# Loads of k, v and part of the weights moved from SyncE's DMA queue to GpSimd's own

## The chip, the cores and the metric

The kernel runs on one core of one Trainium2 chip. The metric is the device time of one execution in microseconds: 828.01 us is the median of three runs of the kernel before (825.59, 828.01 and 830.17 us). Engines are named as the profile names them: PE is TensorE's matmul, PEld its weight load, DVE is VectorE, ACT is ScalarE, POOL is GpSimd, SP is SyncE, which here does nothing but issue DMAs.

## The reference

Two stages follow each other. The first is attention with 4 batches, 12 heads, 448 positions and 64 elements for each head, with a mix over the heads ahead of the softmax and another behind it. The second is a feed-forward layer with a rational activation, on 1792 tokens (4 x 448), width 768 (12 x 64) and 2048 inner columns.

```
scores = einsum('bhij,hg->bgij', scale * (q @ k^T), w_pre)
attn   = softmax(scores)                      # over j
out    = einsum('bgij,..->', attn, w_post) @ v
h      = x @ w_in                             # x: out, heads side by side
g      = (a0 + a1 h + a2 h^2 + a3 h^3) / (1 + |b0||h| + |b1| h^2)
result = g @ w_out
```

The weights w_in and w_out are given as float64; the kernel turns each number into two float32 parts itself (high and low) with integer operations, in pieces of 128 x 384 numbers.

## The kernel before, in words

**Attention.** The 448 rows of a batch are cut into four tiles of 120 rows (one of them 88), 16 tiles in all. For a tile, six QK steps (line 498, one for each pair of heads) write the scores to PSUM, ACT and DVE copy them to SBUF buffers named st (line 238 on DVE and 236 on ACT; six buffers), and a DMA for each head, the shuffle d<-st (line 520, SP's queue), rewrites them so that a partition holds a row and a head. Every pair of ten-row blocks of a tile then makes a group, 92 groups in all, in this chain: the mix ahead of the softmax on PE (line 599, needs all shuffles of the tile); the row maximum nm on DVE (line 605); the exponentials e on ACT (line 614); a guard on POOL that adds 1e-9 to the sums sm (line 621); the reciprocal rr on DVE (line 625); the scaling of the second mixing matrix, krs, on POOL (line 634, two for each group); the mix behind the softmax on PE (line 674), two groups later; and transposes on DVE (line 690). Three times for each tile PE multiplies with v (line 739). The results go to xs and by DMA to x_scr (line 762).

**Weights during attention.** The feed-forward weights with f = 0, 1 and 3 (the list VIA) are prepared while attention runs, 12 pieces: a load cr<-in_w (line 406), steps on ACT, POOL and DVE that write cm, cg and co, and a store w_scr<-co (line 450). The other weights are prepared later, during the feed-forward stage, by the same function put_w.

**Feed-forward.** 64 units of 18 matmuls (line 918), the activation on ACT and DVE, and 18 matmuls (line 1008).

**What sets the order.** A planner (class Plan) places every operation on an engine by assumed durations, due times (at), earliest times (since) and dependencies; the instructions are then issued in that order on each engine, and each engine runs its own list in order. In this planner a DMA on SP has a short duration there and a transfer time (extra) on one queue that serves one transfer after another. All loads and stores but 24 joins of the feed-forward output (line 1059, POOL) and three shuffles (ACT) are issued by SP. SP runs its list in order as well: a load that stands ahead of a shuffle is issued ahead of it.

**Names and lines that the change touches.** The function bulk (line 357) adds a load to the plan; put_k (line 368) loads k of a batch in 6 pieces of 224 KB; put_w (line 401) loads and prepares weights; put_v (line 707) loads v of a batch in four pieces (384 KB, the last one 192 KB). k and v have two buffers each, cr three.

Of the kernel before, what the change touches and what calls it, by code (L numbers as in the profile page):

```python
# [11 lines left out]
I32 = mybir.dt.int32  # L12
# [6 lines left out]
B, H, S, D = 4, 12, 448, 64  # L19
# [18 lines left out]
CV = 384  # L38
# [16 lines left out]
class Plan:  # L55
# [163 lines left out]
def dma(nbytes):  # L219
    return nbytes / 300e3  # L220
# [21 lines left out]
def mixed_attention_then_rational_ffn(ctx: ExitStack, tc, q, k, v, w, wmix, mask, a, b2, out):  # L242
# [3 lines left out]
    nc = tc.nc  # L246
# [5 lines left out]
    add = plan.add  # L252
# [6 lines left out]
    base, after = ctx.enter_context(ExitStack()), ctx.enter_context(ExitStack())  # L259
# [9 lines left out]
    def open_pools(stack, side, sizes):  # L269
# [32 lines left out]
    tau = [T0]  # L302
# [3 lines left out]
    first = {}  # L306
# [61 lines left out]
    def put_k(b, parts, at, gap=0.8):  # L368
        free = R["k"].take()
        n = H // 2 // parts  # L370

        def load(i):
            def fn():
                if i == 0:
                    K[b] = sb["k"].tile([128, H // 2, S], F32, tag="k", name="kk")
                nc.sync.dma_start(out=K[b][:, i * n:(i + 1) * n], in_=k[b, :, i * n:(i + 1) * n])
            return fn

        k_ld[b] = []
# [8 lines left out]
    VIA = (0, 1, 3)  # L388
# [11 lines left out]
    def put_w(f, c, at, since=0.0, g=None):  # L400
# [2 lines left out]

        def load():
            t = sb["cr"].tile([128, CV, 2], I32, tag="cr", name="cr")
            nc.sync.dma_start(out=t.rearrange("p n t -> p (n t)"), in_=w[f, :, sl].bitcast(I32))
            box["hi"], box["lo"] = t[:, :, 1], t[:, :, 0]

        def mag():
# [39 lines left out]
        def store():  # L449
            nc.sync.dma_start(out=w_scr[f][:, :, sl], in_=box["o"].bitcast(F32))  # L450

        ld = add("sp", 0.45, load, [R["cr"].take()], at=at - 5.0, extra=dma(128 * CV * 8), since=max(since, at - 9.0))
        near = lambda i, k: [] if g is None else [posts[min(g + i, len(groups) - 1)][k]]
        o1 = add("act", act(CV), mag, [ld, R["cm"].take(), *near(0, 3)], at=at, late=4.0)
        o2 = add({"dve": 0.32} if g is None else {"pool": 1.54}, 0, clamp, [o1, *near(0, 1)], at=at)
# [251 lines left out]
    def put_v(b, at, gap=8.0):  # L707
        def load(j):
            def fn():
                if j == 0:  # L710
                    V[b] = sb["v"].tile([128, NB, G6, D], F32, tag="v", name="vv")
                sl = slice(j, min(j + 2, NB))
                nc.sync.dma_start(out=V[b][:, sl], in_=v[b, :, sl])
            return fn

        free = R["v"].take()
        v_ld[b] = []
        for i, j in enumerate(range(0, NB, 2)):
            v_ld[b].append(bulk(
                0.63, load(j), [free], after=v_ld[b][:1], at=at + gap * i, nbytes=128 * min(2, NB - j) * G6 * D * 4, since=at + gap * i))  # L720

    Xs, sums = {}, {}

# [76 lines left out]
    for T in range(3, NT):  # L800
        put_q(T, at=tau[first[T - 1]] - LEAD.get(T, 22.0), since=tau[first[T - 1]] - LEAD.get(T, 22.0))
    for b in range(1, B):
        put_k(b, 6, at=tau[first[4 * b - 4]] + 20.0 if b > 1 else tau[first[2]] - 10.0, gap=7.0 if b > 1 else 4.5)
    for b in range(B):
        put_v(b, at=tau[first[4 * b - 4]] + 58.0 if b else 23.0, gap=7.0 if b else 0.7)
    for pr in range(H // 2):
# [353 lines left out]
```

## Time and profile before

| what | value |
|---|---|
| median of 3 runs | 828.01 us (825.59 to 830.17) |
| the profiled execution | 822.94 us, of which the span (first to last instruction) is 821.2 us |
| granted TensorE clock, mean | 0.998 of full speed |
| busy in the span | PE 97%, PEld 73%, DVE 84%, ACT 61%, POOL 27% |
| attention (20 to 340 us) and feed-forward (340 us to the end) | 320 us and 481.2 us |

PE's busy time includes matmuls that run into one another, so a busy PE is not PE at its best rate. A row of the timeline stands for several like instructions in a row: its start and length in us, then in brackets the idle time ahead of it and what ended that.

### The profile page before, as it was taken

What the parts mean: (1) busy time and instruction counts of PE and PEld (TensorE: products, weight loads), DVE (VectorE), ACT (ScalarE), POOL (GpSimd) and SP (SyncE); (2) the same over time, 40 slices, a digit from 0 to 9 for tenths busy, and PEclk for the clock granted to TensorE, in tenths of its full rate; (3) what the DMA queues carried; (4) which work ended last, traced back from release to release, by engine and by line L of the source; (5) the groups of instructions that cost most, each with busy time, mean ns of one, the idle gap of its engine ahead of it and who ended that gap; (6) DMA issues with size and microseconds to landing.
All of it is one profiled execution on the core that took longest, in us unless ns stands there. A gap on an engine that the chain in (4) does not pass through costs nothing.

```text
span 821.2 us, 23269 instructions
## 1 busy us (share of the span) xinstructions
PE 799.4 (97%) x9368; PEld 598.1 (73%) x9368; DVE 692.3 (84%) x1252; ACT 502.0 (61%) x1099; POOL 223.7 (27%) x394
## 2 busy tenths in 40 slices
PE   7899999999999999999999999999999999999998
PEld 2245555554454454689999999999999999999997
DVE  6777788888887888788999998999989998777775
ACT  2557666656665666666777776677657676545632
POOL 2334444434343445611211212222212222100000
PEclk9999999999999999999999999999999999999999
DMA  6777887668877865974733275656467534466314
GB/s 219 254 215 235 259 280 236 209 199 281 266 212 210 269 192 189 352 243 192 257 126 100 75 255 126 188 124 125 84 215 212 152 81 67 94 221 224 128 52 157
DMA packets 72332, 155.46 MB, mean 189 GB/s; under 512 B 12608, under 2 KB 53152, under 8 KB 71072
## 3 DMA queue, kind: packets, MB, share of 16 engines
q1 hardware_dynamic: 68468, 142.47, 52.6%
q0 software_dynamic: 3456, 11.01, 8.2%
q8 instruction: 74, 1.21, 0.6%
q10 hardware_dynamic: 300, 0.48, 0.2%
q14 instruction: 34, 0.28, 0.1%
HBM read 77.49 MB, written 37.75 MB: 140 GB/s over the span
## 4 chain that ended last, share of the span: by engine, by line
PE 87%; DVE 5%; DMA 3%; ACT 2%; issue 1%; POOL 1%; SPq 0%; ACTq 0%; POOLq 0%; DVEq 0%
PE ps_s L918 29%; PE ps_u L1008 10%; PE ps_t L1008 9%; PE ps_a L1008 9%; PE ps_s L498 8%; PE ps_a L674 8%; PE ps_u L599 4%; PE ps_t L599 4%; PE ps_u L739 3%; PE ps_t L739 2%; ACT e L614 2%; DVE nm L605 2%; DMA d<-st 1%; DVE aa L690 1%; DMA kk<-in_k 1%
## 5 line engine op out<-in xcount | busy, mean ns | idle before, releaser
L690 DVE STREAM_TRANSPOSE aa<-ps_a 128x448 f32<-128x448 f32 (+1 forms) x184 | 107.7, 618 | 11.7 <-PE ps_a L674 11.2
L918 PE MATMUL ps_s<-d,w 128*128 128x448 f32 x504 | 107.3, 366 | 0.0
L918 PE MATMUL ps_s<-xs,w 128*128 128x448 f32 x504 | 107.1, 366 | 0.0
L447 POOL TENSOR_TENSOR w<-cm,w 128x384 fp32r<-128x384 f32 x48 | 56.0, 1167 | 171.9 <-ACT w L236 165.0
L918 PEld LDWEIGHTS ps_s<-d,w 128*128 128x128 f32 x504 | 94.3, 188 | 8.8 <-issue 0.7
L918 PEld LDWEIGHTS ps_s<-xs,w 128*128 128x128 f32 x504 | 94.6, 188 | 7.9
L634 POOL TENSOR_SCALAR krs<-kpost,rr 128x64 f32<-128x64 f32 x180 | 80.8, 462 | 69.2 <-DVE rr L625 48.0
L674 PEld LDWEIGHTS ps_a<-e,krs 64*32 64x32 f32 x2880 | 44.9, 106 | 74.7 <-issue 26.6
L674 PE MATMUL ps_a<-e,krs 64*32 64x224 f32 x2880 | 93.2, 355 | 1.5 <-DVE aa L690 0.8
L236 ACT COPY st<-ps_s 120x448 f32<-120x448 f32 (+1 forms) x115 | 57.6, 533 | 57.8 <-PE ps_s L498 30.5
L931 ACT ACTIVATE m<-ps_s,a_sb 128x448 f32<-128x448 f32 x64 | 46.3, 723 | 76.1 <-PE ps_s L918 72.7
L498 PE MATMUL ps_s<-kk,q 64*64 64x448 f32 x696 | 90.2, 548 | 0.3 <-DVE st L238 0.3
L1008 PE MATMUL ps_u<-g,w 128*128 128x448 f32 x336 | 84.1, 366 | 0.0
L1008 PE MATMUL ps_a<-g,w 128*128 128x448 f32 x336 | 84.1, 366 | 0.0
L1008 PE MATMUL ps_t<-g,w 128*128 128x448 f32 x336 | 83.9, 366 | 0.0
L614 ACT ACTIVATE e<-ps_t,nm 128x448 f32<-128x448 f32 x92 | 57.7, 634 | 31.1 <-DVE nm L605 28.0
L614 ACT ACTIVATE e<-ps_u,nm 128x448 f32<-128x448 f32 x88 | 55.2, 633 | 28.9 <-DVE nm L605 24.6
L1008 PEld LDWEIGHTS ps_t<-g,w 128*128 128x128 f32 x336 | 63.1, 188 | 5.3
L1008 PEld LDWEIGHTS ps_a<-g,w 128*128 128x128 f32 x336 | 63.1, 188 | 5.2
L1008 PEld LDWEIGHTS ps_u<-g,w 128*128 128x128 f32 x336 | 63.1, 188 | 5.2
L961 DVE TENSOR_TENSOR sq<-sq,ua 128x448 f32<-128x448 f32 x64 | 41.4, 648 | 19.4 <-ACT ua L958 19.1
L954 ACT ACTIVATE ua<-sq 128x448 f32<-128x448 f32 x64 | 37.1, 580 | 33.9 <-DVE sq L951 33.6
(94 smaller groups left out, 1445.1 us busy)
## 6 DMA issues: line engine op xcount, KB each, us to landing
d<-st SPq DMA_DIRECT2D x144, 210.0 KB
cr<-in_w SPq DMA_DIRECT2D x64, 384.0 KB
d<-x_scr SPq DMA_DIRECT2D x5, 2688.0 KB
xs<-x_scr SPq DMA_DIRECT2D x4, 2688.0 KB
o_scr<-o POOLq DMA_DIRECT2D x24, 448.0 KB, 5.5
d<-st SPq DMA_DIRECT2D x45, 157.5 KB
x_scr<-xs SPq DMA_DIRECT2D x12, 540.0 KB
q<-in_q SPq DMA_DIRECT2D x16, 384.0 KB
```

Of the source, the lines that this page charges most:

```text
L236: eng.copy(o, i)
L447: eng.tensor_sub(t[:, 1, :], box["m"].bitcast(F32), t[:, 0, :].bitcast(F32))
L498: nc.tensor.matmul(box["s"][hh][i0:i1, 0:S], lhsT=Q[T][d, pr, i0:i1], rhs=K[b][d, pr, :], start=True, stop=True)
L599: nc.tensor.matmul(box[r if nt == 2 else 0]["t"][64 * c:64 * c + 64, 0:S], lhsT=kpre[p], rhs=Dt[T][p, kb + c if nt == 2 else kb, :], start ...
L614: nc.scalar.activation(e, box[r]["t"][:, 0:S], AF.Exp, bias=box[0]["nm"][:, r:r + 1], accum_out=box[0]["sm"][:, r:r + 1])
L634: eng.tensor_scalar_mul(box[r]["kr"], kpost, rr)
L674: nc.tensor.matmul(banks[c]["p"][q_:q_ + BT, JH * r:JH * (r + 1)], lhsT=box[r]["kr"][p, m_, :], rhs=box[r]["e"][p, JH * jh:JH * (jh + 1)], ...
L690: nc.vector.transpose(o, src)
L918: nc.tensor.matmul(h[:, 0:S], lhsT=W[fi][:, wi, kk * 128:(kk + 1) * 128], rhs=x[:, kk // 3, xj, kk % 3, :], start=(n == 0), stop=(n == 3 * ...
L931: nc.scalar.activation(new("m"), box["h"], AF.Identity, scale=a_sb[:, 3:4], bias=a_sb[:, 2:3])
L961: nc.vector.tensor_mul(box["vv"], box["vv"], box["rc"])
L1008: nc.tensor.matmul(O[key][:, 0:S], lhsT=W[fi][:, wi, DM + m * 128:DM + (m + 1) * 128], rhs=box["g"][:, gi, :], start=(f == 0 and n == 0), ...
```

## The change

The pieces of k of batches 1 to 3, those of v of batches 1 to 3, and the loads of the 12 weight pieces that are prepared during attention are issued by GpSimd (nc.gpsimd.dma_start) and no longer by SyncE. k of these batches comes in 3 pieces of 448 KB in place of 6 of 224 KB. The planner is told 1.0 us on POOL and 4 us more until the data is there. 33 DMAs are added to POOL's list (9 of k, 12 of v, 12 of weights), and 42 leave SP's list (18, 12 and 12). Batch 0's k and v, and all weights loaded in the feed-forward stage, stay on SP.

```
--- before.py
+++ after.py
@@ -356,6 +356,8 @@
 
     def bulk(dur, fn, deps, at, nbytes, **more):
 
+        if more.pop("by", "sp") == "pool":
+            return add("pool", 1.0, fn, deps, at=at, extra=4.0 + dma(nbytes), **more)
         return add("sp", dur, fn, deps, at=at, extra=dma(nbytes), **more)
 
     def put_q(T, at, since=0.0):
@@ -373,12 +375,12 @@
             def fn():
                 if i == 0:
                     K[b] = sb["k"].tile([128, H // 2, S], F32, tag="k", name="kk")
-                nc.sync.dma_start(out=K[b][:, i * n:(i + 1) * n], in_=k[b, :, i * n:(i + 1) * n])
+                (nc.gpsimd if b else nc.sync).dma_start(out=K[b][:, i * n:(i + 1) * n], in_=k[b, :, i * n:(i + 1) * n])
             return fn
 
         k_ld[b] = []
         for i in range(parts):
-            k_ld[b].append(bulk(0.45, load(i), [free], at=at + gap * i, nbytes=128 * n * S * 4, since=at + gap * i - 4.0, after=k_ld[b][:1]))
+            k_ld[b].append(bulk(0.45, load(i), [free], at=at + gap * i, nbytes=128 * n * S * 4, since=at + gap * i - 4.0, after=k_ld[b][:1], by="pool" if b else "sp"))
 
 
     w_done = {f: [] for f in range(NF)}
@@ -403,7 +405,7 @@
 
         def load():
             t = sb["cr"].tile([128, CV, 2], I32, tag="cr", name="cr")
-            nc.sync.dma_start(out=t.rearrange("p n t -> p (n t)"), in_=w[f, :, sl].bitcast(I32))
+            (nc.gpsimd if f in VIA else nc.sync).dma_start(out=t.rearrange("p n t -> p (n t)"), in_=w[f, :, sl].bitcast(I32))
             box["hi"], box["lo"] = t[:, :, 1], t[:, :, 0]
 
         def mag():
@@ -449,7 +451,7 @@
         def store():
             nc.sync.dma_start(out=w_scr[f][:, :, sl], in_=box["o"].bitcast(F32))
 
-        ld = add("sp", 0.45, load, [R["cr"].take()], at=at - 5.0, extra=dma(128 * CV * 8), since=max(since, at - 9.0))
+        ld = add("pool" if f in VIA else "sp", 1.0 if f in VIA else 0.45, load, [R["cr"].take()], at=at - 5.0, extra=(4.0 if f in VIA else 0.0) + dma(128 * CV * 8), since=max(since, at - 9.0))
         near = lambda i, k: [] if g is None else [posts[min(g + i, len(groups) - 1)][k]]
         o1 = add("act", act(CV), mag, [ld, R["cm"].take(), *near(0, 3)], at=at, late=4.0)
         o2 = add({"dve": 0.32} if g is None else {"pool": 1.54}, 0, clamp, [o1, *near(0, 1)], at=at)
@@ -710,14 +712,14 @@
                 if j == 0:
                     V[b] = sb["v"].tile([128, NB, G6, D], F32, tag="v", name="vv")
                 sl = slice(j, min(j + 2, NB))
-                nc.sync.dma_start(out=V[b][:, sl], in_=v[b, :, sl])
+                (nc.gpsimd if b else nc.sync).dma_start(out=V[b][:, sl], in_=v[b, :, sl])
             return fn
 
         free = R["v"].take()
         v_ld[b] = []
         for i, j in enumerate(range(0, NB, 2)):
             v_ld[b].append(bulk(
-                0.63, load(j), [free], after=v_ld[b][:1], at=at + gap * i, nbytes=128 * min(2, NB - j) * G6 * D * 4, since=at + gap * i))
+                0.63, load(j), [free], after=v_ld[b][:1], at=at + gap * i, nbytes=128 * min(2, NB - j) * G6 * D * 4, since=at + gap * i, by="pool" if b else "sp"))
 
     Xs, sums = {}, {}
 
@@ -800,7 +802,7 @@
     for T in range(3, NT):
         put_q(T, at=tau[first[T - 1]] - LEAD.get(T, 22.0), since=tau[first[T - 1]] - LEAD.get(T, 22.0))
     for b in range(1, B):
-        put_k(b, 6, at=tau[first[4 * b - 4]] + 20.0 if b > 1 else tau[first[2]] - 10.0, gap=7.0 if b > 1 else 4.5)
+        put_k(b, 3, at=tau[first[4 * b - 4]] + 20.0 if b > 1 else tau[first[2]] - 10.0, gap=14.0 if b > 1 else 9.0)
     for b in range(B):
         put_v(b, at=tau[first[4 * b - 4]] + 58.0 if b else 23.0, gap=7.0 if b else 0.7)
     for pr in range(H // 2):
```

The planner orders all engines anew. The order of PE's matmuls is the same before and after.

POOL's list at the groups 8 to 12 (kk and in_k are k, cr and in_w the weights, sm the guard, krs the scaling); before:

```order
L621 TENSOR_SCALAR sm<-sm 128x2
L634 TENSOR_SCALAR krs<-kpost,rr 128x64 x2
L621 TENSOR_SCALAR sm<-sm 128x2
L634 TENSOR_SCALAR krs<-kpost,rr 128x64 x2
L621 TENSOR_SCALAR sm<-sm 128x2
L634 TENSOR_SCALAR krs<-kpost,rr 128x64 x2
L621 TENSOR_SCALAR sm<-sm 128x2
L634 TENSOR_SCALAR krs<-kpost,rr 128x64 x2
L337 MEMSET c_sb 128x1
```

The same groups on POOL in the changed kernel:

```order
L378 DMA kk<-in_k 128x896
L623 TENSOR_SCALAR sm<-sm 128x2
L636 TENSOR_SCALAR krs<-kpost,rr 128x64 x2
L623 TENSOR_SCALAR sm<-sm 128x2
L636 TENSOR_SCALAR krs<-kpost,rr 128x64 x2
L378 DMA kk<-in_k 128x896
L623 TENSOR_SCALAR sm<-sm 128x2
L636 TENSOR_SCALAR krs<-kpost,rr 128x64 x2
L337 MEMSET c_sb 128x1
```

Two DMAs of k stand between the scaling of a group and the guard of the next: the first ahead of the guard of group 9, the second ahead of that of group 11, the first of tile 2.

POOL's list at the groups 51 to 53 (tiles 8 and 9; cm is a step of the weights), before:

```order
L621 TENSOR_SCALAR sm<-sm 128x2
L416 TENSOR_SCALAR cm<-cm 128x384
L634 TENSOR_SCALAR krs<-kpost,rr 128x64
L621 TENSOR_SCALAR sm<-sm 128x2
L634 TENSOR_SCALAR krs<-kpost,rr 128x64 x3
L447 TENSOR_TENSOR co<-cm,co 128x384
L621 TENSOR_SCALAR sm<-sm 128x2
L634 TENSOR_SCALAR krs<-kpost,rr 128x64 x2
```

The same place on POOL in the changed kernel:

```order
L623 TENSOR_SCALAR sm<-sm 128x2
L378 DMA kk<-in_k 128x896
L418 TENSOR_SCALAR cm<-cm 128x384
L623 TENSOR_SCALAR sm<-sm 128x2
L636 TENSOR_SCALAR krs<-kpost,rr 128x64 x2
L408 DMA cr<-in_w 128x768
L636 TENSOR_SCALAR krs<-kpost,rr 128x64 x2
L623 TENSOR_SCALAR sm<-sm 128x2
```

A DMA of k now stands behind the guard of group 51, ahead of the step cm, and a load of weights between the scalings of the groups 51 and 52.

SP's list around the first loads of k of batch 1, before:

```order
L520 DMA d<-st 10x12x448 x3
L376 DMA kk<-in_k 128x448
L520 DMA d<-st 10x12x448 x2
L376 DMA kk<-in_k 128x448
L406 DMA cr<-in_w 128x768
L376 DMA kk<-in_k 128x448 x2
L520 DMA d<-st 10x12x448 x2
L364 DMA q<-in_q 128x768
```

The same place on SP in the changed kernel:

```order
L522 DMA d<-st 10x12x448 x5
L366 DMA q<-in_q 128x768
L522 DMA d<-st 10x12x448 x6
```

The shuffles of a tile now follow one another with nothing between them but a load of q.

## Rows read from the trace of the kernel before

**Rows 1.** The page's chain that ended last, by engine

```profile
PE 87%; DVE 5%; DMA 3%; ACT 2%; issue 1%; POOL 1%; SPq 0%; ACTq 0%; POOLq 0%; DVEq 0%
```

**Rows 2.** Busy time by stretch: length, each engine (instructions), clock, DMA share, GB/s

```profile
20.00:340.00 320.00, 308.14 (x6653) 154.98 (x6646) 262.64 (x484) 196.39 (x530) 134.98 (x303) 0.99 0.76 238
340.00:821.20 481.20, 477.36 (x2612) 438.09 (x2610) 416.70 (x750) 299.62 (x560) 83.16 (x82) 1.00 0.52 156
```

**Rows 3.** Timeline of PE, the mix ahead of the softmax: start, length, idle before

```profile
34.70 0.98 PE L599 MATMUL ps_t<-d,kpre 64*64 64x448 f32 x8 [2.49 <-DMA d<-st]
54.70 0.98 PE L599 MATMUL ps_u<-d,kpre 64*64 64x448 f32 x8 [0.30 <-DMA kk<-in_k]
138.29 0.98 PE L599 MATMUL ps_u<-d,kpre 64*64 64x448 f32 x8 [0.28 <-DMA cr<-in_w]
```

**Rows 4.** The chain of waits at 47 us: start, length, what

```profile
47.26 7.46 DMA kk<-in_k
```

**Rows 5.** Timeline of PE, QK steps of tiles 8 and 12

```profile
160.74 1.21 PE L498 MATMUL ps_s<-kk,q 64*64 64x448 f32 x8
167.34 1.85 PE L498 MATMUL ps_s<-kk,q 64*64 64x448 f32 x8
251.38 1.91 PE L498 MATMUL ps_s<-kk,q 64*64 64x448 f32 x8 [0.33 <-DVE st L238]
```

**Rows 6.** Timeline of ACT, a copy of scores

```profile
251.72 0.53 ACT L236 COPY st<-ps_s 120x448 f32<-120x448 f32 x1 [1.21 <-DMA d<-st]
```

**Rows 7.** Timeline of SP's queue

```profile
162.69 0.50 SPq L713 DMA_DIRECT2D vv<-in_v  x1
163.29 6.19 SPq L520 DMA_DIRECT2D d<-st  x6
```

**Rows 8.** Line 1059, DMAs issued by POOL: ns min/median/max; us to landing

```profile
L1059 POOL DMA_DIRECT2D o_scr<-o x24: 858/872/1063, 500.3 to 716.1; - x24
DMA to landing us min/median/max: 5.0/5.5/11.2
```

**Rows 9.** By line, 20 to 340 us: count | busy, mean ns | idle

```profile
L634 POOL TENSOR_SCALAR krs<-kpost,rr 128x64 f32<-128x64 f32 x177 | 79.0, 460 | 69.2 <-DVE rr L625 48.0 <-PE ps_a L674 9.1 <-PE ps_s L498 4.8
L621 POOL TENSOR_SCALAR sm<-sm 128x2 f32<-128x2 f32 (+1 forms) x90 | 20.9, 232 | 115.0 <-ACT e L614 113.0 <-PE ps_t L599 0.2
L238 DVE COPY st<-ps_s 120x448 f32<-120x448 f32 (+1 forms) x55 | 33.5, 617 | 12.7 <-PE ps_s L498 9.0 <-PE ps_a L674 3.2 <-DMA d<-st 0.2
```

**Rows 10.** Timeline of POOL: groups 10 and 11, group 24, group 51

```profile
57.60 0.86 POOL L634 TENSOR_SCALAR krs<-kpost,rr 128x64 f32<-128x64 f32 x2 [1.56 <-PE ps_a L674]
58.55 0.22 POOL L621 TENSOR_SCALAR sm<-sm 128x2 f32<-128x2 f32 x1
59.84 0.86 POOL L634 TENSOR_SCALAR krs<-kpost,rr 128x64 f32<-128x64 f32 x2 [1.07 <-DVE rr L625]
...
104.44 0.86 POOL L634 TENSOR_SCALAR krs<-kpost,rr 128x64 f32<-128x64 f32 x2 [0.83 <-DVE rr L625]
...
201.72 1.50 POOL L416 TENSOR_SCALAR cm<-cm 128x384 f32<-128x384 f32 x1 [0.22 <-ACT cm L411]
203.20 0.45 POOL L634 TENSOR_SCALAR krs<-kpost,rr 128x64 f32<-128x64 f32 x1
```

**Rows 11.** Timeline of DVE, reciprocal of group 11

```profile
59.53 0.14 DVE L625 RECIPROCAL rr<-sm 128x2 f32<-128x2 f32 x1
```

**Rows 12.** Timeline of PE, the mix behind the softmax of groups 11, 24, 51

```profile
61.53 0.99 PE L674 MATMUL ps_a<-e,krs 64*32 64x224 f32 x32
...
108.62 0.99 PE L674 MATMUL ps_a<-e,krs 64*32 64x224 f32 x32
...
204.48 1.42 PE L674 MATMUL ps_a<-e,krs 64*32 64x224 f32 x32
```

**Rows 13.** The page's DMA queues: packets, MB, share of 16 engines

```profile
q1 hardware_dynamic: 68468, 142.47, 52.6%
q0 software_dynamic: 3456, 11.01, 8.2%
```

More of the change, by code (lines that the diff above doesn't have):

```diff
@@ L357, in bulk @@
     def bulk(dur, fn, deps, at, nbytes, **more):
+        if more.pop("by", "sp") == "pool":
+            return add("pool", 1.0, fn, deps, at=at, extra=4.0 + dma(nbytes), **more)
         return add("sp", dur, fn, deps, at=at, extra=dma(nbytes), **more)
@@ L375, in fn @@
                     K[b] = sb["k"].tile([128, H // 2, S], F32, tag="k", name="kk")
-                nc.sync.dma_start(out=K[b][:, i * n:(i + 1) * n], in_=k[b, :, i * n:(i + 1) * n])
+                (nc.gpsimd if b else nc.sync).dma_start(out=K[b][:, i * n:(i + 1) * n], in_=k[b, :, i * n:(i + 1) * n])
             return fn
@@ L380, in put_k @@
         for i in range(parts):
-            k_ld[b].append(bulk(0.45, load(i), [free], at=at + gap * i, nbytes=128 * n * S * 4, since=at + gap * i - 4.0, after=k_ld[b][:1]))
+            k_ld[b].append(bulk(0.45, load(i), [free], at=at + gap * i, nbytes=128 * n * S * 4, since=at + gap * i - 4.0, after=k_ld[b][:1], by="pool" if b else "sp"))
     w_done = {f: [] for f in range(NF)}
@@ L405, in load @@
             t = sb["cr"].tile([128, CV, 2], I32, tag="cr", name="cr")
-            nc.sync.dma_start(out=t.rearrange("p n t -> p (n t)"), in_=w[f, :, sl].bitcast(I32))
+            (nc.gpsimd if f in VIA else nc.sync).dma_start(out=t.rearrange("p n t -> p (n t)"), in_=w[f, :, sl].bitcast(I32))
             box["hi"], box["lo"] = t[:, :, 1], t[:, :, 0]
@@ L450, in store @@
             nc.sync.dma_start(out=w_scr[f][:, :, sl], in_=box["o"].bitcast(F32))
-        ld = add("sp", 0.45, load, [R["cr"].take()], at=at - 5.0, extra=dma(128 * CV * 8), since=max(since, at - 9.0))
+        ld = add("pool" if f in VIA else "sp", 1.0 if f in VIA else 0.45, load, [R["cr"].take()], at=at - 5.0, extra=(4.0 if f in VIA else 0.0) + dma(128 * CV * 8), since=max(since, at - 9.0))
         near = lambda i, k: [] if g is None else [posts[min(g + i, len(groups) - 1)][k]]
@@ L712, in fn @@
                 sl = slice(j, min(j + 2, NB))
-                nc.sync.dma_start(out=V[b][:, sl], in_=v[b, :, sl])
+                (nc.gpsimd if b else nc.sync).dma_start(out=V[b][:, sl], in_=v[b, :, sl])
             return fn
@@ L719, in put_v @@
             v_ld[b].append(bulk(
-                0.63, load(j), [free], after=v_ld[b][:1], at=at + gap * i, nbytes=128 * min(2, NB - j) * G6 * D * 4, since=at + gap * i))
+                0.63, load(j), [free], after=v_ld[b][:1], at=at + gap * i, nbytes=128 * min(2, NB - j) * G6 * D * 4, since=at + gap * i, by="pool" if b else "sp"))
     Xs, sums = {}, {}
@@ L802, in mixed_attention_then_rational_ffn @@
     for b in range(1, B):
-        put_k(b, 6, at=tau[first[4 * b - 4]] + 20.0 if b > 1 else tau[first[2]] - 10.0, gap=7.0 if b > 1 else 4.5)
+        put_k(b, 3, at=tau[first[4 * b - 4]] + 20.0 if b > 1 else tau[first[2]] - 10.0, gap=14.0 if b > 1 else 9.0)
     for b in range(B):
```

## The prediction

> **What bounds the kernel now.** I read the chain that ended last first: PE holds 87% of the span, all DMAs together 3%, POOL 1% [rows 1]. Then the busy time by stretch [rows 2]: in the feed-forward stage PE is busy for 477 of 481 us, so what attention gains or loses arrives at the end unchanged. In attention, 20 to 340 us, PE is busy for 308.14 of 320 us: 11.9 us of pauses, and that is the room for any gain there, beside matmuls that are stretched without a pause in the profile. Then the timeline of PE, for which of these pauses have SP's queue behind them. The longest is 2.49 us, ahead of the mix of group 5, the first of tile 1, at 34.70 us, and it waits for a shuffle [rows 3]. It stands among batch 0's loads, where the order on SP is the same before and after, so it stays. Two more start a tile's mix late by 0.30 and 0.28 us and are put down to a load of k and one of the weights; what the mix needs is the tile's last shuffle, which landed with them on the same queue [rows 3]. The chain shows how long that queue is: a piece of k issued at 47.26 us landed 7.46 us later [rows 4]. Third, two QK steps late in a tile last 1.85 and 1.91 us where the one before lasts 1.21 [rows 5]; the ACT copy beside the second waits 1.21 us for a shuffle to release an st buffer [rows 6]. On SP one sees why: a load of v, then six shuffles that take 6.19 us to issue [rows 7].
>
> **The change part by part.**
>
> *Loads off SP.* 42 DMAs leave SP's list (18 of k, 12 of v, 12 of weights). With about 0.5 us for each [rows 7] SP has 21 us less to issue. SP's time is not on the chain (0%) [rows 1], so it counts only where a shuffle is late. Those places are: 0.30 at 54.70 us, 0.28 at 138.29 us, 1.85 - 1.21 = 0.64 at 167.34 us, and 1.91 - 1.21 + 0.33 = 1.03 at 251.38 us [rows 3, 5]. Sum 2.25 us. From above the gain is bounded by all pauses in attention without the one that stays, 11.9 - 2.5 = 9.4, and the two stretches, 0.64 + 0.70: 10.7 us. From below by nothing: the transfers still run on the DMA engines that the shuffles use, busy 76% in this stretch [rows 2], and a load that is served beside the shuffles may hold them up as much as one ahead of them. I take 2.25, since those rows name a DMA or the shuffle's buffer and the other pauses name ACT or DVE.
>
> The Trainium skill, "DMA: Bandwidth & Descriptors" (section "Issuing engines are not separate DMA queues"), says that DMAs from any engine run on the same 16 DMA engines and interleave, so that issuing from several engines saves only the issue time. By that rule the sum loses its 2.25 us and would be a loss of 1.3 us. The trace before cannot decide, since it has no stretch of attention with two queues at work.
>
> *Issues on POOL.* 33 DMAs are added. POOL's only DMAs in the trace, 24 joins of 448 KB, take 858 to 1063 ns of POOL each, median 872 [rows 8]; I take that for each of the 33, which makes 28.8 us. POOL idles for 320 - 135 = 185 us of attention [rows 2], mostly in front of the guard (115 us) and of the scaling (69 us) [rows 9]. So the question is only where an issue stands. A group's scaling has to be done before PE's mix behind the softmax. In wide groups there is room: group 24's scaling ends at 104.44 + 0.86 = 105.30 and PE comes at 108.62, 3.3 us later; in tight ones there is little: group 11's ends at 60.70, PE comes at 61.53, 0.8 us [rows 10, 12]. I went through POOL's new list group by group against the timeline of before: 28 of the 33 issues stand in wide groups, with 1.4 us or more to spare, and cost nothing. Five stand at tight ones.
>
> Group 11 is the pattern of four of them. The k load follows group 10's scaling (57.60 + 0.86 = 58.46) and ends at 59.33; the guard (0.22) then runs to 59.55 in place of 58.77. The reciprocal starts at 59.53 in any case [rows 11], since DVE had other work, so it moves by some 0.1 us, which the 0.8 us take up. I put 0.1 us on each, 0.4 in all. The fifth is group 51: the k load stands between its guard and the step cm, which runs from 201.72 to 203.22, with the scaling right behind it at 203.20 and PE at 204.48 already waiting (1.42 us in place of 0.99) [rows 10, 12]. There the whole 0.87 us goes on the path. Cost 1.3 us. The bounds: nothing, if every issue is hidden, and 5 x 1.06 = 5.3 us, if none of the five is.
>
> *Landing of the moved loads.* POOL's DMAs land 5.0 to 11.2 us after issue [rows 8]. The last piece of k of batch 1 is issued behind group 10 and first read at about group 16, six groups of 320 / 90 = 3.6 us later (90 guards in the stretch [rows 9]): 21 us, so it costs nothing; with that cover gone, PE would wait for all of it. The other k, v and weight loads have as many groups or more, and the buffers into which they go are free groups earlier, so that no issue waits on POOL.
>
> *The rest of the plan.* Larger pieces of k carry the same bytes. DVE takes 72 score copies in place of 70 and ACT two fewer; at 617 ns [rows 9] that is 1.2 us of DVE, which idles for 57 us of the stretch [rows 2]: taken at nothing, 1.2 us as its bound. In the feed-forward stage DVE and ACT get another order, behind a PE that never pauses there: nothing.
>
> *Sum.* -2.25 + 1.3 = -0.95 us. The profiled execution took 822.94 us, 821.2 of it span, and would take 822.0. It lies 5.1 us under the median of the runs, 828.01, so for the median I take 828.01 - 0.95 = 827.1 us. A difference under 0.5% (4.1 us) is about what a measurement of this kernel can't tell from none.
>
> **The rivals.**
>
> *Faster: the queue was behind more than the rows name.* Shuffles on time keep the st buffers free, and then ACT and DVE, which run their lists in order, are early as well. At most all 10.7 us go; with the 1.3 us on POOL that is 9.4 us, 818.6 us. For it: the 7.46 us from issue to landing [rows 4], and st buffers that are full in one place at least [rows 6]. Against it: most pauses in the timeline are put down to ACT or DVE and not to a DMA.
>
> *Slower: POOL in the chain.* The guard and the scaling of every group run on POOL; if an issue holds POOL longer than 0.87 us, the tight groups pay. Group 11 has 0.76 us up to its reciprocal and 0.8 us behind it, so an issue of up to 1.5 us is hidden there; group 51 pays at once. With no gain from SP and none of the five hidden it is 5.3 us, 833.3 us. For it: a POOL that lies between ACT's sums and DVE's reciprocal in every group, with DVE waiting in order behind it. Against it: 185 us idle, and 28 of 33 issues in wide groups. It decides from about 1.5 us for one issue.
>
> The Trainium skill, "SBUF — State Buffer" (sections "SBUF: two separate sides" and "A bandwidth-pool intuition that's wrong (but worth ruling out)"), warns that descriptors of DMAs from GpSimd are written by GpSimd itself, which VectorE's two-port operations lock out of the shared port: about 620 ns alone, 3100 ns beside such an operation. The rows agree only in part: beside a busy DVE the 24 joins spread by 0.2 us and not by 2.5 [rows 8]. Had each issue taken the page's 3.1 us, five tight places would pay some 5 x (3.1 - 1.5) = 8 us, an estimate.
>
> *Slower: busier DMA engines.* For each MB, POOL's queue took 8.2 / 11.01 = 0.74% of the engines' time and SP's 52.6 / 142.47 = 0.37% [rows 13]. The moved 13 MB at the first price add 4.9% of 821 us, 40 us, to a stretch of 320 us that stands at 76%: 88%. The shuffles then land later; if each of the 13 tile starts from tile 3 on waits as at 54.70 us, that is 13 x 0.30 = 3.9 us, and with 1.3 on POOL and no gain 833.2 us. Against it: the joins add in memory, which plain loads don't.
>
> *Nothing but a swap.* The engines serve the same bytes, and a shuffle waits beside a load in place of behind it: no gain, 1.3 us of cost, 829.3 us. This is within the same bound as the forecast.
>
> **How the numbers follow.** Forecast and swap together, from 823.9 to 832.1 us: 0.46. The faster rival, all beyond 4.1 us: 0.30, as the pauses leave room but name other engines. POOL in the chain 0.15, busier DMA engines 0.09, both slower by more than 0.5%. Range for 8 in 10: down to 819.0, near the end of the faster rival, and up to 833.5, just over the ends of the slower ones. Faster 0.30, same 0.46, slower 0.24; the likeliest case's own range is 823.9 to 832.1 us.
>
> **What would show it.** Right: the mixes at 54.70 and 138.29 us start without a pause that names a DMA, no QK step takes 1.8 us, DMA issues on POOL take about 0.87 us each, 33 of them, and PE's pauses from 20 to 340 us fall by about a microsecond. Wrong: POOL's issues at 1.5 us or more, PE waiting behind scalings at tight groups, shuffles landing later than before, or pauses that vanish where no DMA was named.

## The result and the profile after

The changed kernel is slower: 838.22 us against 828.46 us (medians of 16 runs each), ratio 1.0106, interval 1.008 to 1.0131. Ratios here are taken over undisturbed runs, so one can differ a little from the ratio of the two medians. The profiled execution has a span of 836.8 us, 15.6 us over the one before. Only part of that is the change: the execution before that was profiled took 822.94 us, 5.5 us less than its median. So where a term is read from these two traces it can be too large by half, and the runs below decide.

By stretch (length; busy us and instructions of PE, PEld, DVE, ACT, POOL; clock; DMA share; GB/s), the changed kernel, cut where the feed-forward stage starts in it:

```profile
20.00:355.60 335.60, 314.18 (x6654) 155.97 (x6655) 263.76 (x486) 195.94 (x528) 153.76 (x337) 0.98 0.73 227
355.60:836.80 481.20, 477.24 (x2612) 437.95 (x2610) 421.06 (x754) 297.73 (x556) 80.77 (x81) 1.00 0.52 155
```

Beside [rows 2], the feed-forward stage takes 481.2 us in both, so all 15.6 us are lost in attention. PE's pauses there are 335.60 - 314.18 = 21.4 us, in place of 11.9; the other 6.0 us are matmuls that last longer. The DMA engines are no busier: 0.73 of a longer stretch, in place of 0.76.

The longer matmuls go with TensorE's granted clock (the third number from the end of a row). It was below full speed in three stretches of 20 us of the changed kernel:

```profile
20.00:40.00 20.00, 17.83 (x224) 6.11 (x228) 13.28 (x24) 9.13 (x26) 5.24 (x15) 0.77 0.80 235
60.00:80.00 20.00, 19.95 (x416) 9.79 (x408) 14.87 (x28) 11.72 (x33) 9.89 (x21) 0.92 0.64 183
280.00:300.00 20.00, 17.85 (x396) 8.85 (x392) 14.67 (x29) 10.97 (x30) 8.15 (x17) 0.91 0.80 261
```

The kernel before had 0.91 in the first of these stretches and 1.00 in the other two:

```profile
20.00:40.00 20.00, 16.33 (x236) 5.64 (x228) 14.25 (x26) 10.13 (x29) 6.11 (x17) 0.91 0.77 253
```

A mean below 1.00 says that a part of the stretch ran at the lower of the clock's two levels, 1.2 GHz in place of 2.4. The differences make 20 x (0.14 + 0.08 + 0.09) = 6.2 us, an estimate, which is about the 6.0. The first 2.8 us of it are not the loads' doing: they stand ahead of the first moved load (42.93 us, shown below), and the kernel with v alone on GpSimd, which loses nothing, has 0.78 in that stretch. The other 3.4 us come after pauses of PE that the kernel before did not have, or had shorter (shown next).

The page's chain that ended last, by engine and by line:

```profile
PE 71%; DMA 5%; DVE 4%; issue 1%; ACT 1%; POOL 0%; SPq 0%; ACTq 0%; DVEq 0%; POOLq 0%
PE ps_s L920 28%; PE ps_u L1010 9%; PE ps_t L1010 9%; PE ps_a L1010 9%; DMA d<-st 5%; PE ps_a L676 4%; PE ps_s L500 3%; PE ps_u L741 2%; PE ps_u L601 2%; PE ps_t L601 2%; PE ps_t L741 2%; DVE nm L607 1%; ACT e L616 1%; DVE aa L692 1%; DVE xs L759 1%
```

Beside [rows 1] the DMAs' share went from 3% to 5% of a longer span, the whole 5% being shuffles, and POOL is at 0%. The chain's pieces (start, length) show single shuffles from issue to landing:

```profile
191.46 7.64 DMA d<-st
203.35 6.44 DMA d<-st
305.23 6.97 DMA d<-st
```

PE's timeline, pauses in attention, the changed kernel:

```profile
53.14 1.04 PE L741 MATMUL ps_u<-aa,vv 64*64 64x90 f32 x40 [1.56 <-issue]
...
58.86 0.98 PE L601 MATMUL ps_u<-d,kpre 64*64 64x448 f32 x8 [2.27 <-DMA d<-st]
...
201.03 0.98 PE L601 MATMUL ps_t<-d,kpre 64*64 64x448 f32 x8 [1.10 <-ACT e L616]
205.30 0.56 PE L741 MATMUL ps_u<-aa,vv 64*64 64x90 f32 x17 [0.95 <-issue]
209.98 0.98 PE L601 MATMUL ps_u<-d,kpre 64*64 64x448 f32 x8 [1.64 <-DMA d<-st]
214.47 1.03 PE L676 MATMUL ps_a<-e,krs 64*32 64x224 f32 x32 [0.17 <-POOL krs L636]
...
263.66 2.02 PE L500 MATMUL ps_s<-kk,q 64*64 64x448 f32 x8 [0.54 <-DVE st L238]
...
294.64 0.47 PE L741 MATMUL ps_t<-aa,vv 64*64 64x90 f32 x12 [2.15 <-issue]
...
351.47 0.47 PE L741 MATMUL ps_u<-aa,vv 64*64 64x120 f32 x9 [1.47 <-issue]
```

Three rows of the kernel before to set beside them:

```profile
196.61 0.54 PE L739 MATMUL ps_u<-aa,vv 64*64 64x90 f32 x16 [0.35 <-issue]
200.23 0.98 PE L599 MATMUL ps_u<-d,kpre 64*64 64x448 f32 x8 [0.57 <-DMA x_scr<-xs]
...
281.81 0.45 PE L739 MATMUL ps_t<-aa,vv 64*64 64x90 f32 x9 [1.59 <-issue]
```

The row at 58.86 us answers to the mix at 54.70 us in [rows 3]: it waited 0.30 us and now waits 2.27. At 209.98 us the first mix of tile 9 waits 1.64 us for a shuffle; before, at 200.23 us, it waited 0.57. These two are 3.0 us of the 9.5 us by which PE's pauses grew. A larger part, 4.2 us, stands in the middle of the v matmuls and waits for nothing that the profile shows ("issue"): 6.1 us in four pauses, in place of 1.9 in two. The DMA records of the two traces say more: each of these six pauses ends 1.3 to 1.7 us after the end of a transfer of 16 KB on q8, the queue that the page calls "instruction", so PE seems to have waited for its own instructions. Whether the moved loads delayed these transfers was not tested. The step of 1.91 us in [rows 5] is still there, at 2.02. Around the mix at 58.86 us, SP's queue and POOL:

```profile
42.72 5.64 SPq L522 DMA_DIRECT2D d<-st  x5
48.41 0.50 SPq L366 DMA_DIRECT2D q<-in_q  x1
56.30 1.66 SPq L522 DMA_DIRECT2D d<-st  x2
```

```profile
42.93 0.78 POOL L378 DMA_DIRECT2D kk<-in_k  x1
...
46.16 0.61 POOL L408 DMA_DIRECT2D cr<-in_w  x1
...
50.65 0.59 POOL L378 DMA_DIRECT2D kk<-in_k  x1
```

Five shuffles of tile 2 are issued from 42.72 to 48.36 us. Beside them POOL issues 448 KB of k and 384 KB of weights, and the mix that needs the last of these shuffles starts at 58.86 us, 10.5 us after its issue. In the kernel before, the last two shuffles of tile 2 were issued by 47.21 us, and the mix, which waited there too, came 7.5 us later, at 54.70:

```profile
45.54 1.67 SPq L520 DMA_DIRECT2D d<-st  x2
```

At tile 9, POOL issues a piece of k ahead of the tile's last six shuffles (POOL, then SP's queue):

```profile
194.51 0.61 POOL L378 DMA_DIRECT2D kk<-in_k  x1
```

```profile
196.83 7.53 SPq L522 DMA_DIRECT2D d<-st  x6
```

What the moved loads cost the two queues (packets, MB, share of 16 engines):

```profile
q1 hardware_dynamic: 62420, 129.49, 46.1%
q0 software_dynamic: 6048, 23.99, 13.8%
```

With [rows 13]: POOL's queue took 13.8% of 836.8 less 8.2% of 821.2 = 48.1 us more of the engines for 12.98 MB, SP's 52.6% of 821.2 less 46.1% of 836.8 = 46.2 us less for the same 12.98 MB. A byte costs the engines almost the same on both, so the loss is not in their load. Last, the landing of the nine loads of k, and all issues on POOL, 20 to 355.6 us (count, busy us, mean ns, idle before):

```profile
DMA to landing us min/median/max: 5.9/7.3/9.1
```

```profile
L408 POOL DMA_DIRECT2D cr<-in_w x12 | 7.2, 598 | 0.2
L715 POOL DMA_DIRECT2D vv<-in_v x12 | 7.2, 597 | 0.2
L378 POOL DMA_DIRECT2D kk<-in_k x9 | 5.5, 615 | 0.6 <-DMA d<-st 0.4
```

There are 33, at 0.60 us and not at the 0.87 us of the joins in [rows 8].

### The profile page after: what moved, and what is told of

Same layout as the page of the kernel before. It is cut to its first block, busy times and chain, and to the rows that moved or that the text cites. A ratio compares the mean times of both kernels' runs of the same rounds, so it can differ in the third digit from the quotient of the medians.

```text
span 836.8 us, 23288 instructions
## 1 busy us (share of the span) xinstructions
PE 804.6 (96%) x9368; PEld 598.8 (72%) x9368; DVE 697.8 (83%) x1258; ACT 499.6 (60%) x1093; POOL 240.1 (29%) x427
## 3 DMA queue, kind: packets, MB, share of 16 engines
q1 hardware_dynamic: 62420, 129.49, 46.1%
q0 software_dynamic: 6048, 23.99, 13.8%
## 4 chain that ended last, share of the span: by engine, by line
PE 71%; DMA 5%; DVE 4%; issue 1%; ACT 1%; POOL 0%; SPq 0%; ACTq 0%; DVEq 0%; POOLq 0%
PE ps_s L920 28%; PE ps_u L1010 9%; PE ps_t L1010 9%; PE ps_a L1010 9%; DMA d<-st 5%; PE ps_a L676 4%; PE ps_s L500 3%; PE ps_u L741 2%; PE ps_u L601 2%; PE ps_t L601 2%; PE ps_t L741 2%; DVE nm L607 1%; ACT e L616 1%; DVE aa L692 1%; DVE xs L759 1%
## 5 line engine op out<-in xcount | busy, mean ns | idle before, releaser
L449 POOL TENSOR_TENSOR w<-cm,w 128x384 fp32r<-128x384 f32 x48 | 53.9, 1123 | 179.2 <-ACT w L236 174.7
L676 PE MATMUL ps_a<-e,krs 64*32 64x224 f32 x2880 | 95.4, 362 | 2.4 <-DVE aa L692 1.3
L500 PE MATMUL ps_s<-kk,q 64*64 64x448 f32 x696 | 92.0, 553 | 1.0 <-DVE st L238 0.5
L933 ACT ACTIVATE m<-ps_s,a_sb 128x448 f32<-128x448 f32 x64 | 46.2, 722 | 73.7 <-PE ps_s L920 70.0
L607 DVE TENSOR_REDUCE nm<-ps_u 128x2 f32<-128x896 f32 (+1 forms) x45 | 47.4, 1054 | 16.0 <-PE ps_u L601 14.4
L500 PEld LDWEIGHTS ps_s<-kk,q 64*64 64x64 f32 x696 | 28.6, 134 | 41.6 <-issue 16.9
```

Source lines behind the costliest of these rows:

```text
L449: eng.tensor_sub(t[:, 1, :], box["m"].bitcast(F32), t[:, 0, :].bitcast(F32))
L500: nc.tensor.matmul(box["s"][hh][i0:i1, 0:S], lhsT=Q[T][d, pr, i0:i1], rhs=K[b][d, pr, :], start=True, stop=True)
L607: nc.vector.tensor_reduce(out=nm[:, 0:nt], in_=box[0]["both"][:, 0:nt, 0:S], axis=AX.X, op=ALU.max, negate=True)
L676: nc.tensor.matmul(banks[c]["p"][q_:q_ + BT, JH * r:JH * (r + 1)], lhsT=box[r]["kr"][p, m_, :], rhs=box[r]["e"][p, JH * jh:JH * (jh + 1)], ...
L933: nc.scalar.activation(new("m"), box["h"], AF.Identity, scale=a_sb[:, 3:4], bias=a_sb[:, 2:3])
```

## The experiments

Theory A at first: a load on a queue of its own gets in beside shuffles that it stood behind on SP's list, and a tile's mix then starts late. Rivals: B, every load costs alike; C, the new order of DVE and ACT; D, the larger pieces; E, GpSimd's issues or descriptors; G, which came up on the way, the second queue as such, wherever the load stands. Each ratio is against the kernel before on the same chip, in five rounds.

**Which loads.** k alone, v alone or the weights alone are issued by GpSimd, the others by SyncE as before.

```
k only:  (nc.gpsimd if b else nc.sync).dma_start(out=K[b]..., 3 pieces);  v and weights: nc.sync
v only:  (nc.gpsimd if b else nc.sync).dma_start(out=V[b]...);  k (6 pieces) and weights: nc.sync
w only:  (nc.gpsimd if f in VIA else nc.sync).dma_start(out=t...);  k (6 pieces) and v: nc.sync
```

> Only the nine k loads (448 KB each) of batches 1 to 3 are on GpSimd's queue; v and the weights stay on SyncE. Theory A (a load on a queue of its own is let in beside the shuffles, where SyncE's list had put it behind those due sooner; the large lateness of the mixes in the changed kernel all stands at loads of k): most of the loss is here, 834 to 838 us, ratio 1.007 to 1.012, with pauses of 1.5 us or more ahead of a mix at 50 to 60 us and at 200 to 235 us. Rival B (every load on GpSimd costs alike): 9 of 33 loads, 9/33 of about 9 us, 831 us. Rival C (the new order of DVE and ACT is what costs): no rule by kind, anywhere from 828 to 838.

> Only the twelve v loads of batches 1 to 3 are on GpSimd's queue; k (in six pieces, as before) and the weights stay on SyncE. Theory A: in the changed kernel no lateness stands at a load of v, so 826 to 830 us, ratio 0.997 to 1.002. Rival B (every load alike): 12 of 33, 831.5 to 832 us, ratio 1.004.

> Only the twelve loads of weights prepared during attention are on GpSimd's queue; k (in six pieces) and v stay on SyncE. Theory A: one of them at 46 us is issued among the shuffles of a tile that is due, the others are not, so 827 to 831 us, ratio 0.999 to 1.004. Rival B (every load alike): 831.5 to 832 us, ratio 1.004.

Measured: k alone 837.39 us, ratio 1.0101 (1.0067 to 1.0135), the whole loss. v alone 828.31 us, 1.0003 (0.9974 to 1.0031): nothing. Weights alone 834.32 us, 1.0063 (1.0035 to 1.0091), more than A expected. Rival B falls on v: twelve loads (nine of 384 KB, three of 192 KB) on GpSimd's queue cost nothing. The parts don't add: 1.01 and 0.6 per cent make 1.06 together.

**Piece size.** k in three pieces, but all loads on SyncE; and the changed kernel with six pieces on GpSimd.

```
all on SyncE:  put_k(b, 6, ..., gap=7.0 if b > 1 else 4.5)   ->   put_k(b, 3, ..., gap=14.0 if b > 1 else 9.0)
on GpSimd:     put_k(b, 3, ..., gap=14.0 if b > 1 else 9.0)  ->   put_k(b, 6, ..., gap=7.0 if b > 1 else 4.5)
```

> The piece size alone: k of batches 1 to 3 in three pieces of 448 KB, all loads on SyncE as before. Theory A (the queue of its own): no loss, 826 to 830 us. Rival D (a piece of 448 KB holds a shuffle up for longer than one of 224 KB, whatever the queue): at least half of the loss stays, 833 us or more, with a late mix at 50 to 60 us.

> The changed kernel with k in six pieces of 224 KB in place of three of 448 KB, all still on GpSimd (42 issues in place of 33). Theory A (bytes in flight beside the shuffles, which are the same): 834 to 840 us, within 3 us of the changed kernel. Rival D (on a second queue the large piece is what holds a shuffle up): 828 to 832 us.

Measured: three pieces on SyncE 828.93 us, ratio 0.9975 (0.994 to 1.0009); six on GpSimd 838.55 us, 1.0101 (1.0064 to 1.0138). D falls on both sides.

**No loads.** The moved loads are left out of the kernel before and of the changed one; k and v of batch 0 and the first three weight pieces are used again, so the output is another. The issues of these loads go with their bytes.

```
+                if b:
+                    K[b] = K[0]      # and V[b] = V[0]; weights: one of the first three pieces
+                    return
```

> The kernel before with the 42 moved loads left out (k and v of batch 0 and the first three weight pieces are used again, so what it computes differs): its list on SyncE has the shuffles and stores alone. This is the most that taking loads away can bring. Theory A: the shuffles land 0.5 us earlier or more and the mixes that wait for one no longer do: 818 to 825 us. Rival F (loads cost the shuffles nothing): 827 to 829 us.

> The changed kernel with its 33 loads left out in the same way: its order of DVE, ACT, POOL and SyncE, without the traffic. Theory A: as fast as the kernel before without its loads, within 0.3%, since the new order costs nothing. Rival C (the new order is what costs): at least half of the loss, 4 us, stays between the two.

Measured: 822.67 us, 0.9939 (0.9912 to 0.9967), and 822.46 us, 0.9932 (0.9903 to 0.9961). The new order of DVE, ACT, POOL and SP costs nothing, which ends C. So the moved loads, issues and bytes together, cost about 6 us on SyncE and 14 to 16 on GpSimd (1.0106 less 0.9932 by the ratios, 838.22 less 822.46 by the medians). With six st buffers, about 6 us is what a better way to load could have won. In the kernel before without its loads PE's busy time in attention stays and the DMA share falls from 0.76 to 0.64:

```profile
20.00:340.00 320.00, 308.87 (x6668) 156.81 (x6661) 263.42 (x488) 197.92 (x531) 137.88 (x308) 0.99 0.64 204
```

In the changed kernel without its loads, PE's step behind group 51's scaling, the place where the prediction saw an issue on the path:

```profile
202.31 1.03 PE L687 MATMUL ps_a<-e,krs 64*32 64x224 f32 x32 [0.20 <-POOL krs L647]
```

**Issues without bytes.** As the changed kernel without loads, but 30 of the 33 places issue a DMA of 8 bytes for each partition into a spare tile.

```
+                    K[b] = K[0]
+                    nc.gpsimd.dma_start(out=junk[:, next(nj)], in_=k[b, :, i * n, 0:2])   # v and weights alike
```

> The issues of the change without their bytes: the changed kernel without its loads (822.5 us), but 30 of the 33 places on GpSimd issue a DMA of 8 bytes for each partition into a spare tile (the first three weight pieces are loaded whole; k and v of batch 0 are used again, so what is computed differs). Theory A: the issues stand mostly in GpSimd's idle time, 822 to 824.5 us. Rival E (GpSimd in the chain between the sums and the scaling): 826 us or more.

Measured: 820.03 us, 0.988 (0.9843 to 0.9917), no slower than without them. The profile shows that POOL did spend the time (count, busy us, mean ns):

```profile
L729 POOL DMA_DIRECT2D junk<-in_v x12 | 7.1, 596 | 0.2
L380 POOL DMA_DIRECT2D junk<-in_k x9 | 5.5, 613 | 0.2
```

At 596 to 613 ns an issue is as long as that of a whole load, and the kernel pays nothing for them. E falls as far as POOL's time goes.

**Another hardware queue.** All 33 loads on ScalarE's queue.

```
-  (nc.gpsimd if b else nc.sync).dma_start(out=K[b]...   +  (nc.scalar if b else nc.sync).dma_start(out=K[b]...   # v, weights alike
-  return add("pool", 1.0, fn, ...                       +  return add("act", 1.0, fn, ...
```

> All 33 loads of the change go on ScalarE's hardware queue in place of GpSimd's own, with the same pieces and due times; GpSimd issues none in attention. Theory A (any queue of its own lets the loads in beside the shuffles): the loss stays, 833 to 842 us, ratio 1.006 to 1.016, with shuffles of 9 us and more from issue to landing. Rival E (it is the descriptors that GpSimd writes, or its issue time): the loss goes, 826 to 830 us.

Measured: 850.5 us, 1.0245 (1.0193 to 1.0297). It doesn't tell A from E as cleanly as meant, since ACT has no idle place for the loads: each issue takes its queue 334 ns, and copies of scores and exponentials stand behind it. The issues of k (ns min/median/max) and, as a group, the copies of scores (count, busy us, mean ns, idle before and what ended it):

```profile
L378 ACTq DMA_DIRECT2D kk<-in_k x9: 334/334/394, 38.5 to 225.5; - x9
...
L236 ACT COPY st<-ps_s 120x448 f32<-120x448 f32 x76 | 38.7, 534 | 59.4 <-PE ps_s L500 25.7 <-issue 14.0 <-DMA d<-st 9.2
```

The copies wait 9.2 us for a shuffle's landing, where all of ACT's copies waited 2.0 us in the kernel before and 6.4 in the changed one, so the shuffles are late here too, without a DMA of GpSimd in attention. How much of the 22 us is theirs and how much ACT's, the run doesn't say.

**Another place.** k alone on GpSimd, each piece due at a tile's start, when the first of the next tile's shuffles are issued; then the same for batches 2 and 3 only, and that once more with all loads on SyncE.

```
-  put_k(b, 3, at=tau[first[4 * b - 4]] + 20.0 if b > 1 else tau[first[2]] - 10.0, gap=...)
+  put_k(b, 3, at=[tau[first[4 * b - 5 + i]] + 0.5 for i in range(3)] if b > 1
+             else [tau[first[1]] + 0.5, tau[first[2]] + 0.5, tau[first[2]] + 8.0])   # later runs: batch 1 as before
```

> As the kernel with k alone on GpSimd's queue (837.4 us, ratio 1.010), but each piece of k is due half a microsecond after a tile's start, when the first and not the last of the next tile's twelve shuffles are issued. Theory A in its narrow form (what costs is a load in flight beside the last shuffles of a tile): most of the loss goes, 826 to 831 us, ratio 0.998 to 1.004. Rival G (a second queue takes its share from the shuffles whenever it has work): 834 us or more.

> As the kernel with k on GpSimd's queue at the tiles' starts (833.5 us, ratio 1.0056), but k of batch 1 goes back to SyncE, at its old due times; six loads of k (batches 2 and 3) stay on GpSimd. In the trace of that kernel 4 of the 5 us that it lost against the kernel before by group 6 stand behind the first piece of batch 1, issued at 34 us among the first tiles. Theory A (the place decides): 828 to 831 us, ratio 0.999 to 1.003. Rival G (a second queue takes its share wherever it works): six ninths of the loss with k alone, 834 us.

> The same pieces and due times of k as in the run beside it (batches 2 and 3 at the tiles' starts, three pieces each), but all loads on SyncE. Tells the queue from the place. Theory A (the place decides): the same time as that run, within 2 us. Rival G (the second queue itself costs): 824 to 829 us, and 3 us or more faster than that run.

Measured: 833.49 us, 1.0056 (1.0022 to 1.009); 834.41 us, 1.0051 (1.0021 to 1.0081); on SyncE 833.33 us, 1.0035 (1.0005 to 1.0066). Half of the loss of k alone goes, and the narrow form of A (only a load beside a tile's last shuffles costs) falls: at a tile's start a load costs too, on GpSimd and, though the interval only just leaves out no loss, on SyncE.

**Place and queue taken apart.** The planner gives a load on SyncE another place, since there its transfer is counted against the shuffles and it yields to those due sooner: k of batch 3 starts at 205, 226 and 230 us of the plan, on GpSimd at 195, 209 and 223. Two kernels swap this: all loads on GpSimd at the planned starts that they have on SyncE, and all on SyncE at those that they have on GpSimd. All have k in three pieces.

```
+    KS = iter([41.77, 47.7, 57.04, 114.71, 136.48, 141.95, 205.42, 225.89, 230.04])   # SyncE's places, for GpSimd
+    KS = iter([39.26, 47.7, 56.97, 112.68, 126.5, 140.5, 195.0, 209.04, 223.0])       # GpSimd's places, for SyncE
+            t = next(KS) if b else at + gap * i
-            ... bulk(0.45, load(i), [free], at=at + gap * i, ..., since=at + gap * i - 4.0, ...
+            ... bulk(0.45, load(i), [free], at=t - 6.0 if b else t, ..., since=t if b else t - 4.0, ...   # SyncE: t - 30.0
```

> All 33 loads stay on GpSimd's queue, with k in three pieces, but each becomes due at the planned start that it has when all loads are on SyncE (k of batch 3 at 205, 226 and 230 us of the plan in place of 195, 209 and 223). Theory A (the place decides: on SyncE the planner puts a load behind the shuffles that are due sooner): the loss goes, 826 to 831 us, ratio 0.997 to 1.003. Rival G (the second queue as such: its DMAs share the engines with the shuffles whenever it works): 834 us or more, ratio 1.007 or more.

> The swap the other way: all loads on SyncE as before, k in three pieces, but each at the planned start that it has on GpSimd's list in the changed kernel, ahead of whatever shuffle is ready then. Theory A (the place decides): as slow as the changed kernel, 834 to 840 us. Rival G (the second queue as such): 826 to 830 us.

Measured, beside the two run already (three pieces of k on SyncE, and the changed kernel):

| ratio to the kernel before | loads on SyncE | loads on GpSimd |
|---|---|---|
| at SyncE's places | 0.9975 (0.994 to 1.0009) | 1.0062 (1.003 to 1.0094) |
| at GpSimd's places | 1.0131 (1.0091 to 1.0172) | 1.0106 (1.008 to 1.0131) |

Only one of the four is as fast as the kernel before: the loads stand where SyncE's plan put them, on SyncE's queue. The place alone costs 1.6 per cent on SyncE, the queue alone 0.9 per cent at the good places; both together cost no more than the bad place alone. By the plain medians (828.93, 833.85 and 841.93 us, beside 827.91, 828.98 and 828.98 of the kernel before) it is 1.4 and 0.5 per cent, so the sizes are rough. Nor do the swaps move the loads alone: the planner orders the other work anew each time, and up to some thirty of DVE's five hundred operations in attention stand elsewhere. The order of the changed kernel was shown to be free; those of the two swaps were not run without loads. Whether GpSimd at the good places is better than at its own isn't certain, since the two intervals overlap. So A and G are each half right, with that reservation.

SP's queue at tile 9 with the loads on SyncE at their own places, and after it with those of GpSimd:

```profile
194.18 7.18 SPq L522 DMA_DIRECT2D d<-st  x6
201.42 1.05 SPq L764 DMA_DIRECT2D x_scr<-xs  x2
202.51 1.90 SPq L378 DMA_DIRECT2D kk<-in_k  x1
```

```profile
202.34 1.46 SPq L381 DMA_DIRECT2D kk<-in_k  x1
203.91 6.02 SPq L527 DMA_DIRECT2D d<-st  x6
209.97 3.74 SPq L770 DMA_DIRECT2D x_scr<-xs  x3
```

In the first the load comes behind the six last shuffles of the tile, in the second ahead of them. With the loads on GpSimd at SyncE's places, POOL and SP at the same place:

```profile
201.14 0.60 POOL L381 DMA_DIRECT2D kk<-in_k  x1
```

```profile
194.93 6.88 SPq L527 DMA_DIRECT2D d<-st  x6
201.86 1.41 SPq L770 DMA_DIRECT2D x_scr<-xs  x2
```

The load is issued while the last of the six goes out, in flight beside them. PE's first mix of tile 9, in the order of the kernels above:

```profile
205.97 0.98 PE L601 MATMUL ps_u<-d,kpre 64*64 64x448 f32 x8 [1.55 <-DMA x_scr<-xs]
```

```profile
215.00 0.98 PE L606 MATMUL ps_u<-d,kpre 64*64 64x448 f32 x8 [2.04 <-DMA d<-st]
```

```profile
209.85 1.77 PE L606 MATMUL ps_u<-d,kpre 64*64 64x448 f32 x8 [4.19 <-DMA d<-st]
```

It is late in all three, most on the second queue. From the end of the issue of the six shuffles (201.36, 209.93 and 201.81 us) to the mix it takes 4.6, 5.1 and 8.0 us: the shuffles take longest to be there where the load has a queue of its own, though in that kernel a load of q follows them on SP's list too. One profile each can't carry the ratios; that is what the rounds are for.

**More st buffers.** The changed kernel and the one before with eight in place of six; then all loads on SyncE, k in three pieces, with eight and with ten.

```
-    open_pools(right, "right", (("st", 6), ("q", 3), ("k", 2)))
+    open_pools(right, "right", (("st", 8), ("q", 3), ("k", 2)))      # and ("st", 8) in the planner's rings; 10 in the last
```

> The changed kernel with eight st buffers in place of six. If late shuffles cost by holding st buffers, so that the copies and the next shuffles of the tile stand still: the loss shrinks by half or more, 826 to 833 us. If only the landing of a tile's last shuffle counts: as the changed kernel, 836 to 841 us.

> The kernel before with eight st buffers. If the six buffers hold its shuffles up as well: 821 to 826 us, ratio 0.992 to 0.998. If not: 0.998 to 1.002.

> All loads on SyncE, k in three pieces of 448 KB, eight st buffers. If the two parts add: 0.9975 x 0.9937 = 0.991, 821 to 823 us. If the pieces give nothing: as with the buffers alone, 824 to 826 us.

> The same with ten st buffers. If the buffers still hold the shuffles up at eight: below the run beside it by 1 us or more, 819 to 822 us. If the DMA engines are what is left: the same as that run within 1 us.

Measured: changed kernel 835.94 us, 1.0086 (1.005 to 1.0122); kernel before 825.17 us, 0.9937 (0.9915 to 0.9959); three pieces and eight 828.53 us, 0.9997 (0.9959 to 1.0036); and ten 829.82 us, 1.0005 (0.9967 to 1.0043). The kernel before with eight buffers beats both kernels. But the buffers don't cure the changed kernel, so a shortage of st buffers isn't its main loss, and together with three pieces of k they bring nothing. In the profile of three pieces with eight buffers, an execution of 833.03 us and so 4.5 us over its median, tile 2 starts later than in the changed kernel (61.76 us against 58.86):

```profile
54.65 1.04 PE L741 MATMUL ps_u<-aa,vv 64*64 64x90 f32 x40 [2.96 <-issue]
61.76 0.98 PE L601 MATMUL ps_u<-d,kpre 64*64 64x448 f32 x8 [3.64 <-DMA d<-st]
```

Why the two parts undo one another stays open: more buffers let shuffles be issued sooner, and the plan moves with them, and no run separates these.

## Why the prediction was wrong, step by step

**What bounds the kernel: right.** PE and attention, with the feed-forward stage unchanged at 481.2 us. The shuffles decide when a tile starts, as the prediction read from [rows 3]. It didn't draw the conclusion that a tile start which already waits has no room for a later shuffle.

**Loads off SP, -2.25 us: wrong, and this is the step that failed.** It counted the issue time that leaves SP and bounded the effect "from below by nothing: the transfers still run on the DMA engines that the shuffles use". But nothing isn't the bound: the term can be a loss. On SP's in-order list the planner put a load behind the shuffles that were due sooner, and with three pieces of k in such places on SyncE the time is that of the kernel before (0.9975). On a queue of its own nothing on a list holds a load behind these shuffles. At the same planned places that made 1.0062: 0.9 per cent by the ratios, some 7 us (4 by the medians), where the bound said nothing. The other part is the place: the plan no longer counts the loads against the shuffles and issues them up to 17 us of the plan earlier. The new orders showed it (a load ahead of group 9's guard, issued at 50.65 us, 8.2 us before the mix that waited for tile 2's shuffles) and were read only for what an issue does to POOL, not for which shuffles the load now ran beside. The whole change measured +9.8 us where the sum had -0.95.

One reading behind this term was wrong as well: that the pauses left over name ACT or DVE. The one of 0.57 us at 200.23 us names a DMA and stands at the first mix of tile 9, where the changed kernel then loses time; two more, 1.9 us together, name "issue".

The Trainium skill, "DMA: Bandwidth & Descriptors" (section "Issuing engines are not separate DMA queues"), cited against the change, points the right way: loads on GpSimd interleave with the shuffles on the same engines. The rule leaves issue time as the only gain, and the prediction made a loss of 1.3 us of it. The runs show 9.8 us.

How late shuffles become 9.8 us is only in part shown. In the two traces the pauses that name a shuffle at tiles 2 and 9 grew by 3.0 us and the lower clock behind pauses cost an estimated 3.4; the 4.2 us more of "issue" pauses stand behind transfers of instructions, and no run tells whether the loads delayed those.

**Issues on POOL, +1.3 us: too high.** An issue takes 0.60 us and not 0.87, and 30 of them without their bytes cost nothing (0.988 beside 0.9932 without). At the fifth tight place PE waits 0.17 us for the scaling (row at 214.47), but the changed kernel without loads has the same wait there (0.20 us, shown with that run), so the issue isn't its cause. The bound of 5.3 us was far.

**Landing of the moved loads, nothing: right.** No pause of PE in the changed kernel's attention names a load of k or v, and k lands 5.9 to 9.1 us after its issue, with groups to spare.

**Rest of the plan, nothing: right.** Without loads both orders take the same time (822.67 and 822.46 us). Larger pieces: nothing on either queue.

**The rivals.** "Busier DMA engines" had the side and the place (late shuffles at tile starts), with 3.9 us for them, but the wrong reason: it took the joins' price for a byte, and the loads cost the engines almost the same on both queues. The engines weren't busier; the shuffles merely landed later. Its chance of 0.09 was too low, because the pauses before were read as what could go and not as what could grow. "POOL in the chain" named the wrong engine, and the faster rival's 9.4 us weren't there to be had: with no loads at all the kernel gains 6 us. "Nothing but a swap" was the nearest in thought, but at tile 9 the shuffles with a load beside them took 8.0 us to the mix, and those with the load behind them 4.6.

## What to carry to other kernels

Before transfers are moved to a second queue, ask which urgent transfer stood ahead of them on the first: an in-order list is also a priority, and a second queue gives it up even if every load keeps its planned place. Where a planner sets the places, check that it charges both queues for the same engines. And bound such a move on the side of loss by the room that the urgent transfers have left (here hardly any, since tiles started late before [rows 3]), not by the issue time that is saved.

## What the runs showed of the hardware that was not expected

A DMA that GpSimd issues takes it 0.60 us both for 448 KB of k and for 8 bytes in each of 128 partitions, where the accumulating joins take 0.87 [rows 8]. For each MB a plain load takes the DMA engines nearly as long on GpSimd's queue (48.1 / 12.98 = 3.7 us) as on SyncE's (46.2 / 12.98 = 3.6 us), though all of GpSimd's traffic before, the joins, stood at 67.3 / 11.01 = 6.1 us. And PE pauses of 1 to 3 us in the middle of the v matmuls that wait for nothing the profile shows ("issue") come in the kernel before (1.59 us), in the changed one (0.95 to 2.15) and with eight buffers (2.96), some near late tiles and some not. Of the 69 pauses over 0.3 us that the traces of all the kernels here put down to "issue" in attention, 66 end 1.3 to 1.7 us after a transfer of 16 KB on the instruction queue q8 has ended. That PE waits there for its instructions is what this suggests; no run tried it.
